# One level of Strassen's scheme for the first expert product, and the experts in 16 units

## The chip, the cores and the metric

The kernel runs on one core of one Trainium2 chip. The metric is the time of one execution on the device in microseconds (us), the median of several runs. Engines are named as in the profile: PE (TensorE, matrix products), PEld (its weight loads), DVE (VectorE), ACT (ScalarE), POOL (GpSimd) and SP (SyncE, which issues most transfers).

## What is computed

Attention of 2 batches and 8 heads of 64 over 1152 positions, with queries averaged in pairs, and behind it four experts whose outputs are weighted and summed:

```python
q_pool = q.reshape(B, H, S // 2, 2, D).mean(axis=3)
attn = softmax(q_pool @ k.T / sqrt(D))          # 2 x 8 heads, 576 x 1152
x = (attn @ v) as 1152 rows of 512              # row = batch and position, column = head and unit
p = domain_probs / domain_probs.sum(-1)
for e in range(4):
    h = np.maximum(x @ w1[e], 0.0)              # 512 -> 1024
    out += p[:, e:e + 1] * (h @ w2[e])          # 1024 -> 512
```

All is float32. A product is made of float32r operands: each factor is split into a high half (a rounded copy) and a low half (what the rounding left), and three products are summed: high by high, high by low, low by high.

## The kernel before

**Heads.** The heads are taken in 8 pairs: n = 0 to 3 are the pairs hp = 0 to 3 of batch 0, n = 4 to 7 those of batch 1. A pair has 9 tiles of 128 query rows (i = 0 to 8; 72 tiles g = 9 n + i in all). The loop over g (L426) gives each engine its instructions in this order: the transposes of tile g (T_chunk, L286) with their copies to aT by ACT (L295) and DVE (L293); the exponentials of tile g+1 on ACT (exps, L272); a part of the product with v (PV_part, L308, into po); the preparation of the next pair's q and k; the scores of tile g+2 (S_chunk, L263) with the scaling on DVE (neg_scores, L266, into sx); then the entries of STAGES. Engines run their instructions strictly in the order in which they are written.

A pair's tiles fall into two groups, grp 0 (256 columns) and grp 1 (320). When the last part of a group's v product is there, finish (L334) multiplies it on DVE by the reciprocal row sums rb into x, copies x to xh on ACT and makes the low half xl on POOL. rb comes from diag_sums (reciprocals on DVE, then dg on POOL, L320 and L324) and spread_sums, a product on PE (pr, L331) that waits for dg. diag_sums of grp 1 stands at i = 8, its spread_sums at i = 1 of the next pair.

**Weights.** w1 and w2 come in 16 half-matrices of 512 x 512. load_weights (L65) issues two transfers on SP for one, split_weights (L103) makes the high half (L98, tensor_scalar) and the low half (L101, tensor_tensor) on POOL.

**Experts.** The rows of x are cut into three chunks of 384. For each expert and chunk, mm1 (L495, matmuls in mm1_ft at L92) goes over 8 slices of 128 FF units with 12 matmuls of 384 columns each (four parts of the inner dimension, three half products), and ACT (L94) and DVE (L95) make the halves of the hidden units. mm2 (L505, matmuls at L515) makes three tiles of 128 rows, each of 24 matmuls of 512 columns over the whole FF dimension, which DVE weights and adds into acc (L518, L520). There are 12 such steps. mm1 of a step is written ahead of mm2 of the step before it. So there are 1152 matmuls of 384 columns and 864 of 512 (the last tile is done in two halves of 256).

**The transition.** mm1 of the first expert and chunk is cut into 32 pieces of three matmuls (fill, L418, tile p1t): four pieces at i = 7 of the last pair, four at i = 8, four behind the loop, and the rest behind the last spread_sums and PV_part. gate_weights (L404) makes the expert weights pw on DVE there.

Of the kernel before, what the change touches and what calls it, by code (L numbers as in the profile page):

```python
# [17 lines left out]
def attention_moe_kernel(ctx, tc, q, k, v, probs, w1, w2, out):  # L18
# [35 lines left out]
    wslot.append(q2all[:, :4096].rearrange("p (z c f) -> p z c f", z=2, c=4))  # L54
    identr = const.tile([P, P], F32R, name="identr")
    nc.vector.tensor_copy(identr, ident)

    stage = [
        kn.rearrange("p h t d -> p (h t d)"), qn.rearrange("p t r d -> p (t r d)"),
        stg, qs.rearrange("p t r d -> p (t r d)"),  # L60
    ]
    stage = [t[:, :1024].rearrange("p (c f) -> p c f", c=2) for t in stage]
    order = [(e, w, hf) for e in range(E) for w in (1, 2) for hf in range(2)]

    def load_weights(j):  # L65
        src = weight_src(*order[j])
        for c in range(2):
            nc.sync.dma_start(stage[2 * (j % 2) + c], src[:, 2 * c:2 * c + 2, :])

    def raw_piece(j, kt):  # L70
        return stage[2 * (j % 2) + kt // 2][:, kt % 2, :]

    ha = [
        k2[0].rearrange("p h s -> p (h s)"), khl.rearrange("p h t z d -> p (h t z d)"),
    ]
    ha = [t[:, j * NC:(j + 1) * NC] for t in ha for j in range(6)]
    ha += [q2all[:, 4096 + j * NC:4096 + (j + 1) * NC] for j in range(4)]
    hbufs = [(ha[0:8], ha[8:16])]
    where = {order[0]: wslot[0], order[1]: wslot[1]}

    seq = [(e, c) for e in range(E) for c in ((0, 1, 2) if e < E - 1 else (0, 2, 1))]

    def mm1_ft(e, c, ft, pt, part=None):
        hh, hl = hbufs[seq.index((e, c)) % 2]
# [482 lines left out]
```

## Time and profile before

| | us |
|---|---|
| median of 3 runs | 682.6 (682.49 to 683.42) |
| profiled execution, span of its instructions | 682.3 |
| PE busy | 663.2 (97%) |
| DVE, ACT, POOL busy | 257.9, 226.1, 201.4 |
| chain that ended last: PE, DVE, ACT | 90%, 4%, 4% |
| share of that chain: w2 products (L515) | 29% |
| x.w1 in the expert stage (L92, tile p) | 27% |

The heads end near 284 us; from there to the end the experts run. PE's busy time is that of a pipelined engine, whose records overlap: the time that a stream of matmuls takes is read from the start of one block to the start of the next, not from the mean duration of one. A wait is read from the idle time ahead of an instruction and the releaser named behind it.

### The profile page before, as it was taken

Reading aid. Unit: us, or ns where it says so; the run is one execution under the profiler, and the core shown is the slowest. Engines: PE = TensorE matmul, PEld = TensorE weight load, DVE = VectorE, ACT = ScalarE, POOL = GpSimd, SP = SyncE. Lnnn points to the kernel's source line nnn. Section 1 sums busy time; section 2 is a strip of 40 time slices with the busy share of each in tenths; the row PEclk is TensorE's granted clock in tenths of the full one; section 3 lists DMA queues with packets and bytes.
Section 4 is the critical chain, followed back from the end, with each engine's and each line's share of the span. In section 5 each row is a group of like instructions: output and inputs, shape, how many; then the busy total and the mean of one; then the engine's idle time right before and its main releaser. Section 6 shows DMA issues by size and latency. Waiting matters only on the chain.

```text
span 682.3 us, 11118 instructions
## 1 busy us (share of the span) xinstructions
PE 663.2 (97%) x4634; PEld 553.6 (81%) x4634; DVE 257.9 (38%) x453; ACT 226.1 (33%) x402; POOL 201.4 (30%) x242
## 2 busy tenths in 40 slices
PE   6899999999999999999999999999999999999998
PEld 5667676767676766798989898989898989898987
DVE  4666666667665765221212121212121212121211
ACT  3666676666666665120101010101020202020200
POOL 3224233332323515391250080440160530310000
PEclk7899999999999999999999999999999999999999
DMA  6715362717172931031030030020030100001011
GB/s 207 197 43 140 96 181 57 202 37 201 39 199 75 239 110 62 1 124 62 2 123 1 0 115 10 31 93 1 0 124 1 42 21 1 0 1 33 14 43 51
DMA packets 26451, 50.84 MB, mean 75 GB/s; under 512 B 2464, under 2 KB 9888, under 8 KB 26400
## 3 DMA queue, kind: packets, MB, share of 16 engines
q1 hardware_dynamic: 26400, 50.12, 26.1%
q8 instruction: 37, 0.61, 0.4%
q14 instruction: 14, 0.11, 0.1%
HBM read 30.97 MB, written 2.36 MB: 49 GB/s over the span
## 4 chain that ended last, share of the span: by engine, by line
PE 90%; DVE 4%; ACT 4%; issue 1%; POOL 0%; ACTq 0%; POOLq 0%
PE p L515 29%; PE p L92 27%; PE spt L263 10%; PE po L308 10%; PE pt L286 6%; ACT sx L272 3%; DVE sx L266 3%; PE pk L236 2%; PE p1t L92 2%; PE pr L331 1%; PE pq L208 1%; PE warm L363 0%; DVE q2all L203 0%; ACT q2all L201 0%; ACT q2all L181 0%
## 5 line engine op out<-in xcount | busy, mean ns | idle before, releaser
L92 PE MATMUL p<-xh,wslot 128*128 128x384 f32 x640 | 166.8, 339 | 1.2 <-DVE q2all L95 1.2
L266 DVE TENSOR_SCALAR_CACHE_REDUCE sx<-spt 128x1152 f32<-128x1152 f32 x72 | 97.7, 1357 | 64.5 <-PE spt L263 64.2
L92 PEld LDWEIGHTS p<-xh,wslot 128*128 128x128 f32 x640 | 116.7, 188 | 1.9 <-DVE q2all L95 1.5
L92 PE MATMUL p<-xl,wslot 128*128 128x384 f32 x320 | 108.3, 338 | 0.0
L272 ACT ACTIVATE sx<-sx,mn 128x1152 f32<-128x1152 f32 x72 | 90.6, 1259 | 25.3 <-DVE sx L266 22.1
L263 PE MATMUL spt<-k,q2all 128*128 128x384 f32 x384 | 86.3, 361 | 1.4 <-DVE sx L266 1.4
L308 PE MATMUL po<-aT,vn 128*64 128x320 f32 (+1 forms) x576 | 85.0, 418 | 0.0
L94 ACT ACTIVATE hb<-p 128x384 fp32r<-128x384 f32 x48 | 23.6, 492 | 161.4 <-PE p L92 158.3
L515 PE MATMUL p<-wslot,hb 128*128 128x512 f32 (+1 forms) x348 | 75.8, 375 | 0.0
L263 PEld LDWEIGHTS spt<-k,q2all 128*128 128x128 f32 x384 | 66.5, 195 | 10.8 <-DVE sx L266 6.1
L515 PEld LDWEIGHTS p<-wslot,hb 128*128 128x128 f32 x348 | 62.2, 188 | 11.7
L295 ACT ACTIVATE aT<-pt 128x640 f32<-128x640 f32 x72 | 50.7, 705 | 55.9 <-PE pt L286 55.8
L286 PEld LDWEIGHTS pt<-ident,sx 64*128 64x128 f32 x1296 | 48.0, 140 | 26.1 <-issue 8.2
L520 DVE SCALAR_TENSOR_TENSOR acc<-p,pw,acc 128x512 f32<-128x512 f32 (+1 forms) x28 | 20.5, 732 | 124.1 <-PE p L515 124.1
L286 PE MATMUL pt<-ident,sx 64*128 64x64 f32 x1296 | 59.2, 231 | 5.8 <-DVE q2all L203 2.4
L92 PEld LDWEIGHTS p<-xl,wslot 128*128 128x128 f32 x320 | 60.0, 188 | 0.4
L94 ACT ACTIVATE k<-p 128x384 fp32r<-128x384 f32 x30 | 14.8, 492 | 130.6 <-PE p L92 130.6
L95 DVE SCALAR_TENSOR_TENSOR hb<-p,hb 128x384 fp32r<-128x384 f32 x48 | 26.8, 558 | 78.1 <-ACT hb L94 78.1
L98 POOL TENSOR_SCALAR wslot<-stg 128x512 fp32r<-128x512 f32 x12 | 7.5, 622 | 161.6 <-PE p L92 84.0
L348 POOL TENSOR_TENSOR xl<-xs,xh 128x256 fp32r<-128x256 f32 (+2 forms) x20 | 13.4, 678 | 133.1 <-ACT xh L347 133.1
L515 PE MATMUL p<-wslot,k 128*128 128x512 f32 x168 | 51.9, 390 | 0.0
L308 PEld LDWEIGHTS po<-aT,vn 128*64 128x64 f32 x576 | 35.3, 136 | 20.3
(107 smaller groups left out, 779.7 us busy)
## 6 DMA issues: line engine op xcount, KB each, us to landing
kab<-k SPq DMA_DIRECT2D x32, 288.0 KB, 4.6
q2all<-q2all SPq DMA_DIRECT2D x28, 256.0 KB, 5.1
vn<-in_v_dram SPq DMA_DIRECT2D x8, 576.0 KB, 7.5
kn<-in_moe_w_dram SPq DMA_DIRECT2D x8, 512.0 KB, 3.7
qn<-in_moe_w_dram SPq DMA_DIRECT2D x8, 512.0 KB, 3.8
stg<-in_moe_w_dram SPq DMA_DIRECT2D x8, 512.0 KB, 3.6
qs<-in_moe_w_dram SPq DMA_DIRECT2D x8, 512.0 KB, 3.9
qn<-in_q_dram SPq DMA_DIRECT2D x7, 576.0 KB, 6.0
```

Of the source, the lines that this page charges most:

```text
L92: nc.tensor.matmul(pt, w[:, a, kt, fs], x[:, kt, cols], start=(j == 0), stop=(j == last))
L94: nc.scalar.activation(hh[ft], pt, AF.Relu)
L95: nc.vector.scalar_tensor_tensor(hl[ft], pt, 0.0, hh[ft].bitcast(F32), ALU.max, ALU.subtract)
L236: nc.tensor.transpose(pt[:, i - f0, :], khl[:, i // KT, i % KT].rearrange("p z d -> p (z d)"), identr)
L263: nc.tensor.matmul(spt[g][:, c, :NC], w, x, start=(j == 0), stop=(j == len(ops) - 1))
L266: nc.vector.tensor_scalar(sx[g % 3].rearrange("p (c x) -> p c x", c=3), spt.pop(g)[:, :, :NC], -INV, None, ALU.mult, ALU.min, accum_out=mn ...
L272: nc.scalar.activation(sx[g % 3], sx[g % 3], AF.Exp, bias=mn[g % 3], scale=-1.0, accum_out=sums[n % 2][:, i:i + 1])
L286: nc.tensor.transpose(pt[:, a, kt - k0, :], sx[g % 3][r, kt * P:(kt + 1) * P], ident[r, r])
L295: nc.scalar.activation(dst, pt, AF.Copy)
L308: nc.tensor.matmul(po[h * HALF:(h + 1) * HALF, :w], vn[n % 2][:, h, kt, :], aT[grp][:, h, kt, :], start=(kt == 0), stop=(kt == KT - 1))
L515: nc.tensor.matmul(pc, h[ft][:, ts_], where[e, 2, ft // 4][:, a, ft % 4, c0:c1], start=(m == 0), stop=(m == len(ops) - 1))
L520: nc.vector.scalar_tensor_tensor(ac, pc, pw[:, tt, e:e + 1], ac, ALU.mult, ALU.add)
```

## The change

**x.w1.** The rows of x are cut into the two batches (576 rows, HT), the inner dimension into heads 0 to 7 by halves (hp 0 and 1, hp 2 and 3), and the FF units of a unit into two slices. That makes x a 2 x 2 matrix of blocks A, w1 of the unit a 2 x 2 matrix B, and seven products of sums of blocks stand for eight (Strassen's scheme in Winograd's form). The sums of x (S1 to S4) are made once, in finish: in pairs 4 to 6 on POOL, in pair 7 on DVE with ACT copies (split_x). The sums of w1 (T1 to T4) are made on POOL for each unit. A product is 12 matmuls of 288 columns: two parts of the inner dimension, three half products, two halves of the 576 rows.

**The chains.** The seven products accumulate in three PSUM tiles of two banks, X, Y and Z. X takes product 0 and, once ACT has copied it (m1), product 2. Y takes product 1 and, once DVE has read it (u1), product 3, then (u2) product 5. Z takes product 4 and, once C22 is read, product 6. C11, C22, C21 and C12 are the four blocks of hidden units, of which ACT, DVE and POOL make the halves.

**Units.** The experts run in 16 units u of two FF slices (j and j+4 of expert e). A unit's mm2 goes over all nine row tiles with six matmuls of 512 columns each and adds each into acc, so acc is added to 144 times. mm1(u+1) is written ahead of mm2(u). Weights come per unit: four transfers for w1, one for w2; ACT makes their high halves, POOL the low ones.

**The transition.** Unit 0 takes the place of fill: product 0 at i = 7, product 2 at i = 8 of the last pair, all others behind the last PV_part. gate_weights moves to pair 1. Tiles of q, k and their preparation are laid into common buffers, which later hold sums of x and the split weights.

```diff
+    HT = NT // 2
+    CW = HT // 2
+    NU = E * 4
...
+    XI = {"S3": 0, "S1": 1, "S2": 2, "S4": 3, "A22": 4}
+
+    def xop(op, z, kt):
+        if op in ("A11", "A12"):
+            return xa[:, int(op == "A12"), z, kt, :]
+        j = XI[op]
+        if kt == 0:
+            return xb[:, j, z, :]
+        if j < 4 or z == 0:
+            return q2all[:, (2 * j + z) * HT:(2 * j + z + 1) * HT]
+        return kk[0][:, 3584:3584 + HT]
...
+    WI = {"B11": 0, "B21": 1, "B22": 2, "T1": 3, "T2": 4, "T3": 5, "T4": 6, "B12": 7}
...
+    def load_w1(u):
+        if u >= NU:
+            return
+        e, j = divmod(u, 4)
+        for a in range(2):
+            src = w1[e, 2 * a * P:2 * (a + 1) * P, :].rearrange("(k p) f -> p k f", p=P)
+            for t in range(2):
+                c = (j + 4 * t) * P
+                nc.sync.dma_start(wf[:, WI[f"B{a + 1}{t + 1}"]], src[:, :, c:c + P])
...
+        g = lambda o: wf[:, WI[o]]
+        for o, a, b in (("T1", "B12", "B11"), ("T2", "B22", "T1"), ("T3", "B22", "B12"), ("T4", "B21", "T2")):
+            nc.gpsimd.tensor_tensor(g(o), g(a), g(b), ALU.subtract)
...
+    WCH = [(0, 2), (2, 4), (4, 6), (6, 7)]
...
+    PRODS = [("X", "A11", "B11"), ("Y", "S2", "T2"), ("X", "A12", "B21"), ("Y", "S3", "T3"),
+             ("Z", "S1", "T1"), ("Y", "A22", "T4"), ("Z", "S4", "B22")]
+
+    def product(u, p, kt, chain, first):
+        _, xo, wo = PRODS[p]
+        for m, (a, z) in enumerate(((0, 0), (0, 1), (1, 0))):
+            for c in range(2):
+                nc.tensor.matmul(
+                    chain[:, c, :CW], w1s[u % 2][:, a, WI[wo], kt, :], xop(xo, z, kt)[:, c * CW:(c + 1) * CW],
+                    start=(first and kt == 0 and m == 0), stop=(kt == 1 and m == 2), skip_group_check=True)
...
+        def split_x(op, kt, c, src, eng):
+            hi, lo = xop(op, 0, kt)[:, c], xop(op, 1, kt)[:, c]
+            if eng is nc.gpsimd:
+                nc.gpsimd.tensor_scalar(hi, src, 1.0, 1.0, ALU.mult, ALU.mult)
+            else:
+                nc.scalar.activation(hi, src, AF.Copy)
+            eng.tensor_tensor(lo, src, hi.bitcast(F32), ALU.subtract)
...
-            x = xs[grp]
+            w, kt = GW[grp], hp % 2
+            c = slice(256 * grp, 256 * grp + w)
+            c1 = slice(HT + 256 * grp, HT + 256 * grp + w)
+            x = xr[:, hp, c1 if b else c]
             nc.vector.tensor_tensor(x, po[:, :w], rb[grp], ALU.mult)
             if b == 0:
-                parts = [(0, 256 * grp, w)]
-            elif grp == 0:
-                parts = [(0, 640, 256)]
+                op = "A12" if hp > 1 else "A11"
+                nc.scalar.activation(xop(op, 0, kt)[:, c], x, AF.Copy)
+                nc.gpsimd.tensor_tensor(xop(op, 1, kt)[:, c], x, xop(op, 0, kt)[:, c].bitcast(F32), ALU.subtract)
+                return
+            a11, a12, a21 = xr[:, kt, c], xr[:, kt + 2, c], xr[:, kt, c1]
+            if hp < 2:
+                nc.gpsimd.tensor_tensor(a11, a11, x, ALU.subtract)
+                if hp == 0:
+                    split_x("S3", 0, c, a11, nc.gpsimd)
+                return
+            eng = nc.vector if hp == 3 else nc.gpsimd
+            eng.tensor_tensor(a11, x, a11, ALU.subtract)
+            split_x("S2", kt, c, a11, eng)
+            eng.tensor_tensor(a21, a21, x, ALU.add)
+            if n == NP - 1 and grp:
+                late.append(lambda: split_x("S1", kt, c, a21, eng))
             else:
-                parts = [(0, 896, 256), (256, 576, 64)]
-            for s0, d0, w in parts:
-                c = slice(d0, d0 + w)
-                nc.scalar.activation(xh[:, hp, c], x[:, s0:s0 + w], AF.Copy)
-                nc.gpsimd.tensor_tensor(xl[:, hp, c], x[:, s0:s0 + w], xh[:, hp, c].bitcast(F32), ALU.subtract)
+                split_x("S1", kt, c, a21, eng)
+            eng.tensor_tensor(a12, a12, a11, ALU.subtract)
+            for op, src in (("A22", x), ("S4", a12)):
+                if n == NP - 1 and grp:
+                    late.append(lambda op=op, src=src: split_x(op, kt, c, src, eng))
+                else:
+                    split_x(op, kt, c, src, eng)
+
+        late = []
...
+            if g == NTL - 1:
+                nc.scalar.activation(UT["m1"], chx[:, :2, :CW], AF.Copy)
...
-            elif i >= 7:
-                fill(4)
+            elif i == 7:
+                chx = ps_s.tile([P, 3, 512], F32, tag="s", name="chx")
+                for kt in range(2):
+                    product(0, 0, kt, chx, True)
+            elif i == 8:
+                for kt in range(2):
+                    product(0, 2, kt, chx, False)
...
+            if (n, i) == (1, 4):
+                gate_weights()
+            if (n, i) == (NP - 2, 2):
+                load_w1(0)
+            if (n, i) == (NP - 2, 4):
+                w1_sums(0)
+            if n == NP - 1:
+                if i == 0:
+                    split_x("S3", 1, slice(0, HT), xr[:, 1, :HT], nc.gpsimd)
+                    load_w2(0)
+                if i < 4:
+                    w1_hi(0, WCH[i:i + 1])
+                    w1_lo(0, WCH[i:i + 1])
+                if i == 3:
+                    load_w1(1)
+                if i == 5:
+                    w1_sums(1)
+        w1_hi(1, eng=nc.gpsimd)
+        w1_lo(1)
+        load_w1(2)
         spread_sums(NP - 1, 1)
         PV_part(NP - 1, 1, 0, KT)
-        gate_weights()
-        fill(32)
-
-    with ExitStack() as mctx:
-        mp = mctx.enter_context(tc.tile_pool(name="mp", bufs=1))
-        ps_m = mctx.enter_context(tc.tile_pool(name="ps_m", bufs=4, space=PSUM))
-        for i in range(3):
-            wslot.append(mp.tile([P, 2, 4, 512], F32R, name=f"wslot{i + 2}"))
-        hb = mp.tile([P, 16, NC], F32R, name="hb")
-        hb = [hb[:, j, :] for j in range(16)]
-        hbufs.append((hb[:8], hb[8:]))
+        chy = ps_t.tile([P, 2, 512], F32, tag="t", name="chy")
+        chz = ps_t.tile([P, 2, 512], F32, tag="t", name="chz")
+        for kt in range(2):
+            product(0, 3, kt, chy, True)
+        nc.scalar.activation(UT["y7"], chy[:, :, :CW], AF.Copy)
+        product(0, 4, 0, chz, True)
+        for fn in late:
+            fn()
+        for kt in range(2):
+            product(0, 1, kt, chy, False)
+        nc.vector.tensor_tensor(UT["u2"], chy[:, :, :CW], UT["m1"], ALU.add)
+        nc.vector.tensor_tensor(UT["u1"], UT["u2"], UT["y7"], ALU.subtract)
+        product(0, 4, 1, chz, True)
+        actx.close()
...
+        def prep_w2(u):
+            if u >= NU:
+                return
+            for sl in range(2):
+                nc.scalar.activation(w2s[u % 2][:, 0, sl], w2f[:, sl], AF.Copy)
+            for sl in range(2):
+                nc.gpsimd.tensor_tensor(
+                    w2s[u % 2][:, 1, sl], w2f[:, sl], w2s[u % 2][:, 0, sl].bitcast(F32), ALU.subtract)
+            load_w2(u + 1)
+
+        def prep_w1(u):
+            w1_hi(u)
+            w1_lo(u)
+            load_w1(u + 1)
...
+        def out_c11(u, chain):
+            hi, lo = hidden(u, "C11")
+            nc.scalar.activation(hi, chain[:, :2, :CW], AF.Relu)
+            nc.vector.scalar_tensor_tensor(lo, chain[:, :2, :CW], 0.0, hi.bitcast(F32), ALU.max, ALU.subtract)
+
+        def out_c(u, name, chain, part):
+            c = UT[name]
+            nc.vector.tensor_tensor(c, chain[:, :, :CW], UT[part], ALU.add)
+            hi, lo = hidden(u, name)
+            nc.scalar.activation(c, c, AF.Relu)
+            nc.scalar.activation(hi, c, AF.Copy)
+            nc.gpsimd.tensor_tensor(lo, c, hi.bitcast(F32), ALU.subtract)
+
+        out_c11(0, chx)
+        out_c(0, "C22", chz, "u2")
+        for kt in range(2):
+            product(0, 5, kt, chy, False)
+        out_c(0, "C21", chy, "m1")
+        for kt in range(2):
+            product(0, 6, kt, chz, False)
+        out_c(0, "C12", chz, "u1")
+        prep_w2(0)
...
+    ps_m = ctx.enter_context(tc.tile_pool(name="ps_m", bufs=1, space=PSUM))
+    ps_2 = ctx.enter_context(tc.tile_pool(name="ps_2", bufs=2, space=PSUM))
...
+    def mm1(u):
+        ch = {n: ps_m.tile([P, 2, 512], F32, tag=n, name="ch" + n.lower()) for n in "XYZ"}
+        done = set()
+
+        def prod(p):
+            n = PRODS[p][0]
+            for kt in range(2):
+                product(u, p, kt, ch[n], n not in done)
+            done.add(n)
+
+        prod(0)
+        nc.scalar.activation(UT["m1"], ch["X"][:, :, :CW], AF.Copy)
+        prep_w2(u)
+        prod(1)
+        nc.vector.tensor_tensor(UT["u1"], ch["Y"][:, :, :CW], UT["m1"], ALU.add)
+        prod(2)
+        out_c11(u, ch["X"])
+        prep_w1(u + 1)
+        prod(3)
+        nc.vector.tensor_tensor(UT["u2"], ch["Y"][:, :, :CW], UT["m1"], ALU.add)
+        prod(4)
+        out_c(u, "C22", ch["Z"], "u2")
+        prod(5)
+        out_c(u, "C21", ch["Y"], "m1")
+        prod(6)
+        out_c(u, "C12", ch["Z"], "u1")
...
+    def mm2(u):
+        e, j = divmod(u, 4)
+        h, w = hb[u % 2], w2s[u % 2]
+        for tt in range(NQT):
+            ts_ = slice(tt * P, (tt + 1) * P)
+            ops = [(sl, a, b) for sl in range(2) for a, b in ((0, 0), (0, 1), (1, 0))]
+            split = u == NU - 1 and tt == NQT - 1
+            for c0, c1 in ((0, 256), (256, 512)) if split else ((0, DM),):
+                pt = ps_2.tile([P, 512], F32, tag="m", name="p2")
+                pc, ac = pt[:, :c1 - c0], acc[:, tt, c0:c1]
+                for m, (sl, a, b) in enumerate(ops):
+                    nc.tensor.matmul(pc, h[:, a, sl, ts_], w[:, b, sl, c0:c1], start=(m == 0), stop=(m == len(ops) - 1))
+                if u == 0:
+                    nc.vector.tensor_scalar(ac, pc, pw[:, tt, e:e + 1], None, ALU.mult)
+                else:
+                    nc.vector.scalar_tensor_tensor(ac, pc, pw[:, tt, e:e + 1], ac, ALU.mult, ALU.add)
...
+    for u in range(NU):
+        if u + 1 < NU:
+            w1_sums(u + 2)
+            mm1(u + 1)
+        mm2(u)
```

## Rows read from the trace of the kernel before

**Rows 1.** The page, parts 1 and 2: PE's busy share and its granted clock.
```profile
PE 663.2 (97%) x4634; PEld 553.6 (81%) x4634; DVE 257.9 (38%) x453; ACT 226.1 (33%) x402; POOL 201.4 (30%) x242
...
PEclk7899999999999999999999999999999999999999
```

**Rows 2.** The chain in order of time: start us, us, engine, tile, line, count.
```profile
278.82 4.84 PE po L308 x36
283.67 10.80 PE p1t L92 x60
295.63 17.22 PE p L92 x96
312.85 16.34 PE p L515 x72
329.18 16.96 PE p L92 x96
...
646.02 33.00 PE p L515 x168
```

**Rows 3.** Timeline 255 to 300 us: start us, us, engine, instruction, [idle before it <-releaser].
```profile
269.80 0.33 PE L92 MATMUL p1t<-xh,wslot 128*128 128x384 f32 x1
...
270.17 0.49 ACT L94 ACTIVATE k<-p1t 128x384 fp32r<-128x384 f32 x1 [1.42 <-PE p1t L92]
...
270.69 0.56 DVE L95 SCALAR_TENSOR_TENSOR khl<-p1t,k 128x384 fp32r<-128x384 f32 x1 [3.00 <-ACT k L94]
...
271.31 0.47 PE L286 MATMUL pt<-ident,sx 64*128 64x64 f32 x8 [0.72 <-DVE khl L95]
...
278.06 0.76 PE L331 MATMUL pr<-dg,ones 128*64 128x320 f32 x4 [1.27 <-POOL dg L324]
```

**Rows 4.** Groups by shape, PE and weight loads: count, busy us, mean ns, idle before.
```profile
L515 PE MATMUL p<-wslot,hb 128*128 128x256 f32 x48 | 5.9, 283 | 0.0
...
L92 PEld LDWEIGHTS p<-xl,wslot 128*128 128x128 f32 x320 | 60.0, 188 | 0.4
```

**Rows 5.** Groups by shape, DVE and ACT.
```profile
L170 DVE TENSOR_TENSOR khl<-kn,khl 128x576 fp32r<-128x576 f32 x1 | 0.8, 759 | 1.3 <-ACT khl L169 1.3
L170 DVE TENSOR_TENSOR khl<-kn,khl 128x256 fp32r<-128x256 f32 x1 | 0.4, 426 | 0.5 <-ACT khl L169 0.5
...
L295 ACT ACTIVATE aT<-pt 128x640 f32<-128x640 f32 x72 | 50.7, 705 | 55.9 <-PE pt L286 55.8
L347 ACT ACTIVATE xh<-xs 128x256 fp32r<-128x256 f32 x12 | 4.8, 403 | 6.6 <-DVE xs L338 6.6
```

**Rows 6.** Windows: length, busy us of PE, PEld, DVE, ACT, POOL, clock, DMA.
```profile
312.60:329.00 16.40, 16.40 (x74) 13.60 (x73) 2.06 (x3) 0.49 (x1) 0.00 (x0) 1.00 0.03 12
346.00:362.50 16.50, 16.50 (x74) 13.65 (x73) 2.06 (x3) 0.49 (x1) 6.11 (x7) 1.00 0.27 85
```

**Rows 7.** Groups by shape, POOL.
```profile
L101 POOL TENSOR_TENSOR wslot<-qn,wslot 128x512 fp32r<-128x512 f32 x14 | 18.0, 1289 | 1.2
...
L348 POOL TENSOR_TENSOR xl<-xs,xh 128x256 fp32r<-128x256 f32 x12 | 8.8, 734 | 104.9 <-ACT xh L347 104.9
L98 POOL TENSOR_SCALAR wslot<-qn 128x512 fp32r<-128x512 f32 x14 | 8.7, 623 | 0.0
```

**Rows 8.** Timeline 238 to 251 us: finish of pair 6, first group, and what follows.
```profile
241.44 0.42 DVE L338 TENSOR_TENSOR xs<-po,rb 128x256 f32<-128x256 f32 x1
...
245.21 0.61 POOL L324 TENSOR_SCALAR dg<-ident,rs 128x128 f32<-128x128 f32 x1
...
247.86 0.71 PE L331 MATMUL pr<-dg,ones 128*64 128x320 f32 x4
```

**Rows 9.** Windows at the start, columns as in rows 6.
```profile
4.00:8.00 4.00, 2.19 (x15) 1.69 (x13) 2.14 (x5) 1.97 (x4) 0.74 (x1) 1.00 0.87 279
8.00:12.00 4.00, 2.89 (x11) 2.45 (x11) 2.28 (x3) 0.85 (x2) 0.80 (x1) 0.56 0.50 152
...
24.00:28.00 4.00, 3.34 (x33) 2.65 (x32) 2.57 (x4) 2.61 (x5) 0.00 (x0) 1.00 0.92 219
```

More of the change, by code (lines that the diff above doesn't have):

```diff
@@ L53, in attention_moe_kernel @@
     q2 = [t[:, :2048].rearrange("p (z s x) -> p z s x", z=2, s=2) for t in q2]
[L54 to L84, printed above, removed]
-        cols = slice(c * NC, (c + 1) * NC)
-        w = where[e, 1, ft // 4]
-        fs = slice((ft % 4) * P, (ft % 4 + 1) * P)
-        ops = [(kt, a, x) for kt in range(NKT) for a, x in ((0, xh), (0, xl), (1, xh))]
-        last = len(ops) - 1
-        for j, (kt, a, x) in enumerate(ops):
-            if part is None or kt == part:
-                nc.tensor.matmul(pt, w[:, a, kt, fs], x[:, kt, cols], start=(j == 0), stop=(j == last))
-        if part is None or part == NKT - 1:
-            nc.scalar.activation(hh[ft], pt, AF.Relu)
-            nc.vector.scalar_tensor_tensor(hl[ft], pt, 0.0, hh[ft].bitcast(F32), ALU.max, ALU.subtract)
@@ new lines, in attention_moe_kernel, with flat, w1_hi, w1_lo @@
+    WCH = [(0, 2), (2, 4), (4, 6), (6, 7)]
+    def flat(t):
+        return t.rearrange("p o k f -> p (o k f)")
+    def w1_hi(u, parts=WCH, eng=None):
+        if u >= NU:
+            return
+        for a, b in parts:
+            dst, src = flat(w1s[u % 2][:, 0, a:b]), flat(wf[:, a:b])
+            if eng is None:
+                nc.scalar.activation(dst, src, AF.Copy)
+            else:
+                eng.tensor_scalar(dst, src, 1.0, 1.0, ALU.mult, ALU.mult)
+    def w1_lo(u, parts=WCH):
+        if u >= NU:
+            return
+        for a, b in parts:
+            nc.gpsimd.tensor_tensor(flat(w1s[u % 2][:, 1, a:b]), flat(wf[:, a:b]),
+                                    flat(w1s[u % 2][:, 0, a:b].bitcast(F32)), ALU.subtract)
@@ new lines, in load_w2 @@
+    def load_w2(u):
+        if u < NU:
+            e, j = divmod(u, 4)
+            nc.sync.dma_start(w2f, w2[e].rearrange("(s j p) d -> j p s d", s=2, p=P)[j])
+    UT = {n: xr[:, (0, 2)[j // 2], (j % 2) * HT:(j % 2 + 1) * HT] for j, n in enumerate(("m1", "u1", "u2", "y7"))}
+    UT |= {n: xr[:, (1, 3, 1)[j], (0, 0, 1)[j] * HT:((0, 0, 1)[j] + 1) * HT] for j, n in enumerate(("C22", "C21", "C12"))}
+    UT = {n: t.rearrange("p (c x) -> p c x", c=2) for n, t in UT.items()}
+    PRODS = [("X", "A11", "B11"), ("Y", "S2", "T2"), ("X", "A12", "B21"), ("Y", "S3", "T3"),
+             ("Z", "S1", "T1"), ("Y", "A22", "T4"), ("Z", "S4", "B22")]
@@ new lines, in attention_moe_kernel @@
+    ov = out.rearrange("(b p t) c -> b t p c", b=B, p=HALF)
+    def mm2(u):
+        e, j = divmod(u, 4)
+        h, w = hb[u % 2], w2s[u % 2]
[10 more added lines that the diff above has]
+                    nc.vector.tensor_scalar(ac, pc, pw[:, tt, e:e + 1], None, ALU.mult)
+                else:
+                    nc.vector.scalar_tensor_tensor(ac, pc, pw[:, tt, e:e + 1], ac, ALU.mult, ALU.add)
+                if u == NU - 1:
+                    for a in range(2):
+                        b, t = divmod(2 * tt + a, NQT)
+                        eng = nc.scalar if split and a else nc.sync
+                        eng.dma_start(ov[b, t][:, c0:c1], acc[a * HALF:(a + 1) * HALF, tt, c0:c1])
```

140 lines of the change are left out of this document (33 added, 107 removed).

## The prediction

> **What bounds the kernel now.** I read the page's busy shares first: PE is busy for 97% of the span and its granted clock is full in every slice but the first two [rows 1]. That can still hide waits, so the chain of waits in order of time comes next. From 295.63 us on it is PE alone, in blocks that follow each other without a gap: 96 matmuls of x.w1 in 16.96 us, 72 of the w2 product in 16.34 us [rows 2]. There are 11 blocks of the first kind after the transition (the first takes 17.22 us) and 12 blocks' worth of the second. So behind 295.63 us only PE instructions count: 176.7 ns for one of 384 columns (16.96/96), 227 ns for one of 512 (16.34/72). Between 265 and 295 us, where the last heads hand over to the experts, the rows show waits: PE stands 1.27 us for POOL's dg and 0.72 us for DVE [rows 3]. This stage has to be walked through by hand. The heads before it (tiles g = 0 to 70) are a loop of PE, DVE and ACT that the change touches only where finish, POOL and the weights go.
>
> **The pace at 288 columns.** The change makes 16 x 84 = 1344 matmuls of 288 columns out of 12 x 96 = 1152 of 384: 387,072 columns for 442,368, seven eighths. The trace has no matmul of 288 columns with 128 x 128 weights. Its nearest rows: 384 columns take 176.7 ns; 256 columns take 120 ns (the last block is 33.00 us for 120 of 512 columns and 48 of 256 [rows 2, 4]: (33.00 - 120 x 0.227)/48 = 0.120). On the line between them 288 columns take 134.2 ns, and that is my value; parallel to the slope between 384 and 512 columns it would be 139 (176.7 - 96 x 0.394), and in proportion to the 227 ns of 512 columns 128. I keep 128 to 139. One x.w1 unit is then 84 x 134.2 = 11.27 us, its w2 product 54 x 227 = 12.26 us, a period of 23.5 us.
>
> Each of these matmuls has its own weight load, and the 48 of 256 columns did too; at 120 ns apiece the load is hidden. The Trainium skill ("TensorE: Matmul & The Clock Gate", Part 3, "The mechanism") says that a weight load overlaps matmuls in flight only where the row groups differ. All loads here take all rows, so by it the 192 additional loads, 188 ns each in the trace [rows 4], would lie bare: +36 us, some 700 us in all. The trace disagrees, since 256 columns and a load fit in 120 ns; I give that a chance under 0.01.
>
> **Units 1 to 15.** They replace 11 blocks: 15 x 11.27 = 169.1 us for 11 x 16.96 = 186.6 us: **-17.5 us**, if PE never waits. The w2 products stay 864 matmuls of 512 columns: 0.
>
> Does PE wait? The chains X, Y, Z are read between products that accumulate into them again. A product is 12 matmuls, 1.61 us. A reader starts some 0.37 us after the last matmul's start (269.80 to 270.17) and PE follows a reader's end by 0.06 us (271.25 to 271.31) [rows 3]. A DVE add of 576 elements takes 0.76 us [rows 5], an ACT copy about 0.65 us (0.70 for 640 [rows 5]). With a unit's start as 0: ACT reads X into m1 from 1.85 to 2.5, product 2 needs it at 3.22; DVE's u1 reads Y from 3.45 to 4.2, product 3 comes at 4.83; u2 reads it from 6.7 to 7.45 (behind the low half of C11), product 5 comes at 8.05; C22 reads Z from 8.3 to 9.05, product 6 comes at 9.66. Every hand-over has about 0.6 us to spare. Behind the unit, the accumulation of the w2 product has 1.36 us a tile (6 x 227 ns) and two banks, against 0.75 us of DVE (three of them, one cut off, are 2.06 us [rows 6]). DVE's 108 more accumulations (144 for 36) lie there too. POOL per unit: four sums of 256, 1792 + 1024 + 1728 columns of low halves at 1.29 us per 512 and 0.73 per 256 [rows 7], about 14.4 us of 23.5. ACT: about 8.6 us. All of it is used one unit later. So I cost these at 0; what is late next, if the cover goes, is the DVE add.
>
> **The heads.** finish of pair 6 (hp = 2, b = 1) puts eleven POOL instructions where there was one (xl, 0.73 us): seven tensor_tensor, four tensor_scalar. At 256 columns that is 7 x 0.70 + 4 x 0.42 = 6.6 us (0.734 a tensor_tensor with its gap hidden; a tensor_scalar between 0.31, half of the 0.62 for 512, and 0.62 [rows 7]). Behind them on POOL stands dg of the second group, and PE's spread (pr) waits for dg with everything behind it. In the trace x is ready at 241.86, dg ends at 245.82, pr starts at 247.86 [rows 8]: 2 us to spare. After: 241.95 + 6.6 + 1.8 (dg) = 250.3: PE stands **+2.4 us** (bounds 0.9, if they run at 0.31 and 0.62, to 3.5). The longer chain of the second group (7.6 us) has 12 us until its dg is needed. gate_weights, moved from the transition to pair 1, is 2 us of DVE in a loop that DVE can hold up: **+0.2** (0 to 1). ACT's four copies for w1_hi in pair 7 fit in its idle time there: 0. The DMAs issued on SP (four of 128 KB per unit, and w2's one) have a period each: 0.
>
> **The transition.** PE in the times of the old trace: product 0 begins where the 12 matmuls of the first filling did (the last of them stands at 269.80 [rows 3], so 269.8 - 11 x 0.177 = 267.8 at the latest) and takes 1.6 us to 269.3; transposes and attention product of the last tile go to some 270.5. Product 2 accumulates into X, which ACT first copies to m1, behind its copy of aT: 271.2. So product 2 is 271.3 to 272.9. Then PE has nothing until pr. In pair 7 finish runs on DVE: x, then seven instructions of 0.43 us with ACT copies of 0.40 between them [rows 5], from 270.95 to 275.7; the sums' reciprocals follow on DVE, dg on POOL, and pr starts at 278.1, as it did (278.06 [rows 3]). But the old kernel had 24 more matmuls to put there: PE now stands for 5.2 us instead of 1.27. pr and the last attention product end at 283.67, as before [rows 2]. Products 3, 4 (first half), 1, 4 (second half) are 36 matmuls, 4.8 us, to 288.5; S2's last low half is ready at 285.9. Product 5 waits until DVE, behind S1, A22 and S4, has read u2: 289.25; product 6 until C22 is read: 291.5 to 293.1. The first unit of the loop starts between 293.1 and 294.2 (a chain's banks may still be read by C12); I take 293.7 for 295.63: **-1.9 us**. The columns saved here (60 matmuls of 8.1 us for 60 of 10.8) mostly turn into waits.
>
> Two costs go on top. First, in both groups of that finish DVE runs seven instructions with both operands in SBUF while POOL works on the sums and halves of w1; the old trace shows no such pair beside each other. Bounds: 0, or one POOL instruction each, 4 x 0.70 in the first group, 4 x 1.29 in the second [rows 7]. Nearest to a row is neither; I take a third, **+2.5 us**. The Trainium skill ("SBUF — State Buffer", on the shared port pair) says that DVE and GpSimd lock one port pair for a whole instruction and that the loser blocks; by it the sum would be nearer the upper end, +6. No row here shows it. Second, the clock. Its mean was 0.56 from 8 to 12 us, after 4 us in which PE was busy for 2.19, and 1.00 again from 24 us [rows 9]; later waits of 0.7 to 1.3 us did not lower it [rows 1, 3]. A stand of 5.2 us is longer than any in the trace. At the half level (1.2 instead of 2.4 GHz) the attention product behind it (4.84 us) would take up to twice as long. **+2.0 us** (0 to 5).
>
> **Sum**, against the profiled span: -17.5 + 2.4 + 0.2 - 1.9 + 2.5 + 2.0 = -12.3 us on 682.3 us: 670.0. The median of the runs is 0.3 us above that span: about **670 us**. The tail (last accumulate, two transfers) keeps its length.
>
> **Rivals.**
> (a) No port conflict and no fall of the clock: 4.5 us less, about 665.5. For it: waits up to 1.3 us left the clock alone. Chance 0.22.
> (b) The hand-overs take part of the slack: 0.3 us a unit, or a pace of 138 ns (1260 x 4 ns = 5 us): 673 to 681. Chance 0.20.
> (c) Slower. PE waits in each unit for the DVE reads of the chains (u1, u2, C22). This decides from 12.3/15 = 0.82 us a unit, that is when each of the three reads ends some 0.9 us later than worked out (0.6 spare and 0.27 more). It would come if such an add, one operand in PSUM and one in SBUF, had to wait for a POOL instruction of 1.29 to 1.42 us: three waits of (1.3 - 0.6) make 2.1 us a unit, 670 + 31 = 701; with half of that, 686. Against it: the accumulations, of the same kind of operands, take 2.06 us for three whether POOL is idle or busy for 6.11 us [rows 6]. Chance 0.12.
> (d) The gain vanishes between these, within 0.2%: 0.03.
> (e) A pace near 128 ns and no wait in the transition: below 662. Chance 0.03.
>
> The forecast itself (667 to 673) has 0.40. **Range**: (a), (b) without its upper end and the forecast lie in 662 to 679, about 0.8. A measurement of this kernel can tell about 0.2%, 1.4 us, from no change. Faster by more than that: 0.40 + 0.22 + 0.20 + 0.03 = 0.85; within it 0.03; slower 0.12.
>
> **What the new profile would show.** The product line with 1344 matmuls, 132 to 136 ns from start to start; blocks of 84 in 11.3 us and 54 in 12.3 us in the chain, with no releaser named between them. If DVE adds or POOL stand between blocks, (b) or (c). pr of pair 6 waiting about 2.4 us for dg. A stand of PE of some 5 us ahead of the last pr, and whether the granted clock of the windows behind it falls below 1.00. The first block of 84 starting 3 to 7 us after 293.7. The prediction is wrong if the pace at 288 columns is not on the line between its neighbours, or if any hand-over waits in each of 15 units: 0.1 us there is 1.5 us in the sum.

## The result, and the profile after

The changed kernel takes 674.28 us (674.15 to 676.63), the kernel before 683.01 us (682.49 to 684.11) in the same runs: a ratio of 0.987, interval 0.9849 to 0.9891. It is faster by about 9 us, 1.3%. The forecast was 670, its range 662 to 679. The profiled executions are not the median ones: 674.8 us of span belong to the slowest of four runs (676.63 us, mean granted clock 0.982), while the three others have spans of 672.4 to 672.5 us and clocks of 0.994 to 0.995, and the span of 682.3 us before fits the slowest of its runs, 684.11 us.

The page of the changed kernel, shares and granted clock (the rows of before are [rows 1]):

```profile
PE 644.4 (95%) x4808; PEld 531.2 (79%) x4808; DVE 363.9 (54%) x571; ACT 310.4 (46%) x523; POOL 323.5 (48%) x346
...
PEclk7899999999999999898999999999999999999999
```

PE lost 19 us of busy time, the span only 7.5 (682.3 to 674.8). The 8s in the middle of the clock's row are new. The chain in order of time answers [rows 2]:

```profile
283.54 5.82 PE po L332 x36
...
302.49 2.54 POOL w2s L546 x2
305.05 4.26 DMA qsf<-in_moe_w_dram
312.52 3.12 PE chy L135 x12
315.64 1.85 PE chz L135 x12
317.50 12.28 PE p L625 x54
329.77 1.58 PE chx L135 x12
...
339.36 1.60 PE chz L135 x12
340.96 12.26 PE p L625 x54
```

Two things are to be seen. From 317.5 us on it is PE alone again: seven products in 11.19 us (329.77 to 340.96), the w2 product in 12.26. That pattern holds for units 2 to 15. But in unit 1 the chain leaves PE: it runs over POOL's w2s and a transfer. That unit, from 299.61 (timeline, next) to 317.50, took 17.9 us.

```profile
299.61 1.57 PE L135 MATMUL chx<-xa,kk 128*128 128x288 f32 x10 [0.94 <-ACT hb L569]
```

The waits of PE name what else is new:

```profile
PE pr L355 <- POOL dg L348: 7.2, 2, 4.4
PE chy L135 <- DVE xr L604: 4.7, 1, 4.7
```

So the 7.5 us between the two profiled spans come about like this. The first unit of the loop starts at 299.61 instead of 295.63: +4.0. x.w1 in the loop takes 17.9 + 14 x 11.19 = 174.6 us for 11 blocks with 186.8 us: -12.2. The w2 products stay at 196.2 us. What is left behind the last accumulation grew by some 0.8 us. Together -7.4. The price of the clock is in these numbers, not beside them.

### The profile page after: what moved, and what is told of

Its sections match the earlier page's. It is cut to its first block, busy times and chain, and to the rows that moved or that the text cites. A ratio compares the mean times of both kernels' runs of the same rounds, so it can differ in the third digit from the quotient of the medians.

```text
span 674.8 us, 11945 instructions
## 1 busy us (share of the span) xinstructions
PE 644.4 (95%) x4808; PEld 531.2 (79%) x4808; DVE 363.9 (54%) x571; ACT 310.4 (46%) x523; POOL 323.5 (48%) x346
## 4 chain that ended last, share of the span: by engine, by line
PE 85%; DVE 6%; ACT 5%; POOL 2%; issue 1%; DMA 1%; ACTq 0%; POOLq 0%; DVEq 0%
PE p L625 29%; PE chy L135 11%; PE spt L287 11%; PE po L332 10%; PE chz L135 7%; PE chx L135 7%; PE pt L310 6%; DVE sx L290 3%; ACT sx L296 3%; PE pk L260 2%; PE pr L355 1%; DMA qsf<-in_moe_w_dram 1%; PE pq L232 1%; PE warm L414 0%; POOL xb L364 0%
## 5 line engine op out<-in xcount | busy, mean ns | idle before, releaser
L625 PE MATMUL p<-w2s,hb 128*128 128x512 f32 (+1 forms) x870 | 198.9, 388 | 0.1
L625 PEld LDWEIGHTS p<-w2s,hb 128*128 128x128 f32 x870 | 161.8, 188 | 33.0 <-DVE acc L629 0.3
L629 DVE SCALAR_TENSOR_TENSOR acc<-p,pw,acc 128x512 f32<-128x512 f32 (+1 forms) x136 | 101.5, 746 | 81.6 <-PE p L625 81.6
L287 PE MATMUL spt<-kk,q2all 128*128 128x384 f32 x456 | 101.5, 360 | 1.3 <-DVE sx L290 1.3
L287 PEld LDWEIGHTS spt<-kk,q2all 128*128 128x128 f32 x456 | 79.2, 195 | 11.5 <-DVE sx L290 6.8
L116 POOL TENSOR_TENSOR kk<-kq,kk 128x512 fp32r<-128x512 f32 x64 | 72.0, 1156 | 10.8 <-ACT kk L108 10.8
L570 POOL TENSOR_TENSOR hb<-xr,hb 128x576 fp32r<-128x576 f32 x48 | 68.7, 1435 | 17.3 <-ACT hb L569 17.1
L135 PE MATMUL chx<-xa,kk 128*128 128x288 f32 x384 | 56.4, 296 | 1.5 <-ACT hb L569 0.9
L135 PEld LDWEIGHTS chx<-xa,kk 128*128 128x128 f32 x384 | 53.5, 188 | 3.6 <-issue 1.5
L317 DVE COPY aT<-pt 128x512 f32<-128x512 f32 x72 | 49.0, 680 | 3.6 <-PE pt L310 3.5
```

The lines of the kernel that those rows point to most:

```text
L116: nc.gpsimd.tensor_tensor(flat(w1s[u % 2][:, 1, a:b]), flat(wf[:, a:b]), flat(w1s[u % 2][:, 0, a:b].bitcast(F32)), ALU.subtract)
L135: nc.tensor.matmul(chain[:, c, :CW], w1s[u % 2][:, a, WI[wo], kt, :], xop(xo, z, kt)[:, c * CW:(c + 1) * CW], start=(first and kt == 0 and ...
L287: nc.tensor.matmul(spt[g][:, c, :NC], w, x, start=(j == 0), stop=(j == len(ops) - 1))
L317: nc.vector.tensor_copy(dst, pt)
L570: nc.gpsimd.tensor_tensor(lo, c, hi.bitcast(F32), ALU.subtract)
L625: nc.tensor.matmul(pc, h[:, a, sl, ts_], w[:, b, sl, c0:c1], start=(m == 0), stop=(m == len(ops) - 1))
```

## The experiments

Three waits of PE stand in the trace: 2.8 us for dg of pair 6, 4.4 us for dg of pair 7, 4.7 us in unit 1. Three runs take away one each, by order alone. All times of a kernel are compared by ratio to the kernel before on the same chip (0.987 for the changed kernel), and the spans of the profiled executions by their own rows. A difference of spans compares two single executions, so the ratios say what a move is worth and the rows say where.

### Unit 1's wait: w2 of unit 0 prepared earlier

```diff
         out_c11(0, chx)
+        prep_w2(0)
         out_c(0, "C22", chz, "u2")
...
         out_c(0, "C12", chz, "u1")
-        prep_w2(0)
```

> Only prep_w2(0) is moved: from behind unit 0's last output to behind C11, so that POOL is through with w2's low halves of unit 0, and SP issues the transfer of unit 1's w2, some 8 us earlier. Theory: the 4.7 us for which PE waits in unit 1 (product 5 for u2) is this transfer seen through ACT (w2's copy stands ahead of C11's relu) and DVE (C11's low half stands ahead of u2). Then the wait goes, and with it the fall of the clock behind it: the first unit of the loop takes 11.3 us instead of 17.9, 668 us in all. Rival: the order on ACT and DVE alone does it in the first unit; then the wait stays above 2 us and the time above 671 us.

Measured: 671.87 us (668.59 to 673.1), ratio 0.9812 (0.9776 to 0.9848); span 669.2, 5.6 less. By the ratio it is 4 us less (0.0058 x 683), and the runs lie 4.5 us apart. The expected 668 us, 6.3 less, are reached by unit 1 itself (6.5, below), not by the span and not by the median. The wait for u2 is no longer in the list, and the chain shows unit 1 as PE alone:

```profile
300.45 1.83 PE chx L135 x12
...
310.28 1.60 PE chz L135 x12
311.88 12.26 PE p L625 x54
```

Unit 1 takes 11.43 us (300.45 to 311.88) instead of 17.9: the wait and the low clock behind it were 6.5 us. The rival falls: the same order on ACT and DVE is harmless once the transfer is early. The first unit starts 0.8 us later, though (300.45 for 299.61). POOL's low halves of w2 now lie beside DVE's u1 of unit 0, an add with both operands in SBUF: it takes 1.51 us for 0.76 in the changed kernel, and product 6 of unit 0 waits 1.02 us for 0.27. Timeline of this run:

```profile
294.38 3.03 POOL L546 TENSOR_TENSOR w2s<-qsf,w2s 128x512 fp32r<-128x512 f32 x2 [5.50 <-ACT w2s L544]
294.76 1.51 DVE L531 TENSOR_TENSOR xr<-xr 128x576 f32<-128x576 f32 x1
...
297.66 1.06 PE L135 MATMUL chz<-xb,kk 128*128 128x288 f32 x6 [1.02 <-DVE xr L566]
```

How the wait of unit 1 was passed on is read from the timeline of the changed kernel:

```profile
302.47 2.54 POOL L546 TENSOR_TENSOR w2s<-qsf,w2s 128x512 fp32r<-128x512 f32 x2
...
305.05 7.89 SPq L122 DMA_DIRECT2D qsf<-in_moe_w_dram  x2
...
309.32 1.15 ACT L544 ACTIVATE w2s<-qsf 128x512 fp32r<-128x512 f32 x2 [6.85 <-DMA qsf<-in_moe_w_dram]
...
310.38 0.63 ACT L561 ACTIVATE hb<-chx 128x576 fp32r<-128x576 f32 x1
...
311.04 0.76 DVE L562 SCALAR_TENSOR_TENSOR hb<-chx,hb 128x576 fp32r<-128x576 f32 x1 [7.16 <-ACT hb L561]
311.72 0.75 DVE L604 TENSOR_TENSOR xr<-chy,xr 128x576 f32<-128x576 f32 x1
...
312.52 1.68 PE L135 MATMUL chy<-xb,kk 128*128 128x288 f32 x6 [4.68 <-DVE xr L604]
```

The one buffer of raw w2 is free only when POOL is through with unit 0's low halves (305.01); SP's transfer then lands at 309.3; ACT's copy of w2 stands ahead of C11's relu, C11's low half ahead of u2 on DVE, and product 5 waits for u2. In unit 2 and later the same transfer has a whole w2 product, 12.26 us, to land.

### Pair 6: dg ahead of the sums of x on POOL

```diff
-            eng.tensor_tensor(a11, x, a11, ALU.subtract)
+            if n == NP - 2 and grp == 0:
+                held.append(lambda: sums_x(n, grp, kt, c, x, a11, a12, a21, nc.gpsimd))
+                return
...
             for fn, dn, *args in STAGES.get(i, []):
                 fn(n + dn, *args)
+            while held:
+                held.pop(0)()
```

(sums_x is the rest of finish, unchanged.)

> In pair 6, first group, the eleven POOL instructions of finish are written behind dg instead of ahead of it. Theory: PE's 2.8 us wait for dg goes, and the lower clock behind it (mean 0.67 from 252 to 256 us): 4 us less, 670.3 us. Rival: the loop of the heads gives the time back, because POOL is then late for the second group's dg or the low halves of w1: 1 us less or nothing.

Measured: 673.26 us, ratio 0.984 (0.9825 to 0.9854); span 671.0. The wait for dg of pair 6 is gone; that of pair 7 is where it was:

```profile
PE pr L355 <- POOL dg L348: 4.4, 1, 4.4
```

The first unit of the loop starts at 296.24 in this run's timeline, 3.4 us earlier. The span shows 3.8 us, the ratio 2 us (0.003 x 683), and the intervals of the two ratios overlap (0.9849 to 0.9891 for the changed kernel). The 3.4 us are made of three parts. pr starts 2.9 us earlier (248.09 for 250.98). From pr to X's first product it is 21.0 us here (to 269.13), 21.4 in the changed kernel (to 272.40), where the clock was low behind the wait, and 19.9 in the run of the next section, in which the same wait stands and the clock stayed at 1.00; both runs with all moves, further down, have 21.0 too. So the loop of the heads does give part of the wait back, some 1.1 us (21.0 - 19.9), and the low clock cost some 1.5 (21.4 - 19.9): the rival was right in part.

### Pair 7: dg ahead of DVE's chain

```diff
-            eng.tensor_tensor(a11, x, a11, ALU.subtract)
+            if n == NP - 1 and grp == 0:
+                held.append(lambda: sums_x(n, grp, kt, c, x, a11, a12, a21, nc.vector))
+                return
...
+            while held:
+                held.pop(0)()
```

> In pair 7, first group, DVE's chain of sums is written behind the reciprocals of diag_sums instead of ahead of them. Theory: dg is ready some 4 us earlier, PE's 4.4 us wait shrinks below 0.5 us and the clock behind it stays at 1.00: 6 us less, 668.3 us. DVE's chain now lies beside POOL's work on unit 1's w1 halves. Rival (port conflict): the seven DVE instructions, 0.42 us each while POOL was idle, take up to 1.3 us each beside POOL, S2 comes late, PE waits ahead of product 1, and half of the gain is lost: 671 us.

Measured: 672.16 us, ratio 0.9814 (0.9795 to 0.9833), 3.8 us less; span 668.1. Of the span's 6.7 us, 2.1 are there ahead of the edit: X's first product starts at 270.26 for 272.40. pr of pair 6 accounts for 0.7 of them (250.32 for 250.98); the other 1.5 come behind it, where the clock stayed at 1.00 in this execution (0.67 in the changed kernel's), though PE had waited the same 2.80 us:

```profile
250.32 0.76 PE L355 MATMUL pr<-dg,ones 128*64 128x320 f32 x4 [2.80 <-POOL dg L348]
252.00:256.00 4.00, 4.00 (x52) 2.69 (x51) 2.34 (x4) 2.69 (x5) 3.09 (x4) 1.00 0.25 72
```

(The second line is a window, columns as in [rows 6]; the clock is the number before the last two.) From X's first product to the first unit of the loop (292.45) it is 22.2 us for 27.2: 5.0 us from the edit, expected 6. pr waits 0.89 us instead of 4.38 (expected: below 0.5), the last v product is back at 4.85 us (5.82), and DVE's chain now lies beside POOL. Timeline of this run:

```profile
274.09 0.39 DVE L390 TENSOR_TENSOR xr<-xr 128x256 f32<-128x256 f32 x1
...
274.96 0.84 DVE L364 TENSOR_TENSOR q2all<-xr,q2all 128x256 fp32r<-128x256 f32 x1 [0.48 <-ACT q2all L363]
275.51 1.01 POOL L348 TENSOR_SCALAR dg<-ident,rs 128x128 f32<-128x128 f32 x1
275.72 0.41 DVE L392 TENSOR_TENSOR xr<-xr 128x256 f32<-128x256 f32 x1
...
276.49 2.65 POOL L110 TENSOR_SCALAR kk<-kq 128x512 fp32r<-128x512 f32 x4
276.58 0.76 PE L355 MATMUL pr<-dg,ones 128*64 128x320 f32 x4 [0.89 <-POOL dg L348]
276.62 0.76 DVE L364 TENSOR_TENSOR q2all<-xr,q2all 128x256 fp32r<-128x256 f32 x1 [0.48 <-ACT q2all L363]
...
277.30 0.82 DVE L397 TENSOR_TENSOR xr<-xr 128x256 f32<-128x256 f32 x1
278.05 0.83 DVE L364 TENSOR_TENSOR kk<-xr,q2all 128x256 fp32r<-128x256 f32 x1
```

In the changed kernel the seven instructions, with both operands in SBUF, took 0.42 to 0.43 us each while POOL was idle. Here four take 0.76 to 0.84 us beside POOL's dg and its split of w1 and the last, at 278.80, 0.61; two keep 0.39 and 0.41, and beside the second of these it is POOL's part of dg that takes 1.01 us for 0.60. So the conflict is real, at some 0.4 us an instruction, on one side or the other. DVE's side of it costs nothing visible, since PE has the last v product to do meanwhile. POOL's side falls on dg itself: some 0.4 of the 0.89 us for which pr still waits. Theory and rival each were right in part: the wait is gone but for 0.89 us, the conflict is there, and half of the gain was not lost.

### PE kept busy in the wait

```diff
+        for j in range(30):
+            nc.tensor.matmul(chx[:, 2, :CW], w1s[0][:, 0, 0, j % 2, :], xa[:, 0, 0, j % 2, :CW], ...)
         spread_sums(NP - 1, 1)
```

> Nothing is moved; 30 matmuls of 288 columns whose results nobody reads (third bank of X's tile) are put where PE stands ahead of the last pr. Theory: the wait for dg itself stays, but PE is busy in it and the granted clock stays at 1.00: the last attention product takes 4.84 us again instead of 5.82, and pr 0.8 instead of 1.3: 1.5 us less, 672.8 us. Rival: the clock falls for another reason than PE's standing, and the time stays at 674.3 us or grows.

Measured: 675.64 us, ratio 0.9865 (0.9841 to 0.9889); span 673.6. The windows show what was expected, and a second fall of the clock behind it. First the changed kernel, then this run (columns as in [rows 6]; the clock is the number before the last two):

```profile
252.00:256.00 4.00, 4.00 (x34) 3.06 (x32) 1.56 (x3) 1.81 (x4) 3.54 (x3) 0.67 0.10 29
276.00:280.00 4.00, 1.83 (x12) 1.59 (x12) 2.78 (x9) 1.55 (x4) 0.00 (x0) 1.00 0.00 0
280.00:284.00 4.00, 1.79 (x8) 0.91 (x10) 0.20 (x2) 0.41 (x1) 3.62 (x7) 0.75 0.02 4
284.00:288.00 4.00, 4.00 (x28) 1.98 (x26) 0.00 (x0) 0.03 (x1) 4.00 (x5) 0.83 0.26 76
...
313.00:317.00 4.00, 4.00 (x22) 4.00 (x21) 1.11 (x2) 1.83 (x3) 4.00 (x5) 0.61 0.67 191
```

```profile
280.00:284.00 4.00, 3.57 (x28) 2.67 (x28) 0.42 (x3) 0.44 (x1) 3.40 (x6) 1.00 0.00 0
284.00:288.00 4.00, 4.00 (x31) 1.91 (x27) 0.00 (x0) 0.00 (x0) 4.00 (x5) 1.00 0.23 66
...
308.00:312.00 4.00, 1.61 (x7) 1.61 (x8) 2.18 (x3) 3.45 (x8) 4.00 (x4) 0.63 0.11 12
312.00:316.00 4.00, 4.00 (x19) 4.00 (x19) 0.76 (x1) 2.03 (x3) 4.00 (x4) 0.52 0.77 250
```

With PE busy the clock stays at 1.00, the last v product takes 4.87 us instead of 5.82 and the first unit starts 25.7 us behind X's first product (272.62 to 298.29) instead of 27.2: the expected 1.5 us. So at this place it was PE's standing that lowered the clock, as far as one execution shows it: in the five other traces that keep the wait of 4.38 us the clock fell behind it each time. But behind unit 1's wait, which this run leaves in place, the clock was low for longer than before: the unit took 17.98 us for 17.89, though its wait was shorter (3.88 us for 4.68). What one fall costs is therefore not a constant. Behind pair 7's wait pr and the last v product together took 1.4 to 2.2 us more than the 5.6 us at the full clock, in five traces; unit 1, less its wait and the 11.43 us that it takes without one, lost 1.8 to 2.7 us in four. The span is 1.2 us shorter than the changed kernel's; the medians can't tell the two apart.

### All three moves, and the output on two queues

The edits above together, the two of finish as one:

```diff
+            if n >= NP - 2 and grp == 0:
+                held.append(lambda: sums_x(n, grp, kt, c, x, a11, a12, a21, nc.vector if hp == 3 else nc.gpsimd))
+                return
```

> The three moves together: w2(0) prepared early, dg ahead of finish's sums in pairs 6 and 7. Theory: the three waits lie behind each other in time and add up: 2.8 + 4.4 - 0.9 (left in pair 7) + 4.7 = 11.0 us, and each lowered clock behind them cost 1 to 1.7 us: 14 to 16 us less than the changed kernel, 659 to 661 us, a ratio to the kernel before of 0.965 to 0.968. Rival: removing one wait lengthens the next (POOL is the engine behind all of them): then less than 10 us, above 664 us.

Measured: 661.82 us, ratio 0.9686 (0.967 to 0.9701); span 659.3. Between the two profiled executions the span is 15.5 us shorter; by the ratios the moves are worth 12.6 us (0.0184 x 683), short of the expected 14 to 16, and the median is 0.8 us above the expected 659 to 661. Of the three waits only 0.9 us of pair 7's is left, as expected; product 6 of unit 0 waits 1.06 us for 0.27, as with the early preparation alone; and the granted clock is full behind the start:

```profile
PEclk7999999999999999999999999999999999999999
```

By the ratios the single moves gave 4.0, 2.0 and 3.8 us, 9.8 in all, and together they gave no less. So the waits simply followed each other, and none hid another.

The second kernel also issues every second output transfer of the last unit from ACT:

```diff
-                        eng = nc.scalar if split and a else nc.sync
+                        eng = nc.scalar if a else nc.sync
```

> As the three moves together, and of the last unit's output transfers every second one is issued by ACT instead of SP. Theory: the tail behind the last accumulation is 3.6 us in the changed kernel for 2.8 us in the kernel before because 22 transfers queue up on SP in 12 us (0.68 us each); with half of them the tail is 2.8 us again: 0.5 to 0.8 us less than without it. Rival: the tail is the transfer itself: no difference.

Measured: 661.59 us, ratio 0.9681 (0.9666 to 0.9695); span 659.9. From the end of the last accumulation to the end of the span it is 3.2 us (656.67 to 659.9) for 3.6 without (655.68 to 659.3): 0.4 us less in the traces, less than expected, and not to be told in the medians. The expectation counted 22 transfers; there are 20. It also took 0.68 us for the price of an issue, but that is the pace of the accumulations, two transfers every 1.36 us; a single issue takes 0.47 to 0.54 us. Only at the end does SP fall behind. The last accumulation and the last issue, first in the changed kernel, then here:

```profile
670.76 0.48 DVE L629 SCALAR_TENSOR_TENSOR acc<-p,pw,acc 128x256 f32<-128x256 f32 x1 [0.62 <-PE p L625]
671.76 0.54 SPq L634 DMA_DIRECT2D out_dram<-acc  x1
```

```profile
656.19 0.48 DVE L637 SCALAR_TENSOR_TENSOR acc<-p,pw,acc 128x256 f32<-128x256 f32 x1 [0.63 <-PE p L633]
656.70 0.47 SPq L642 DMA_DIRECT2D out_dram<-acc  x1
```

The last issue starts 0.52 us behind the end of the last accumulation in the changed kernel and 0.03 us behind it here. What makes up the rest of the longer tail stays open. Both kernels beat the changed one by about 12 us and the kernel before by 21.

### The slack of a hand-over

```diff
+        for _ in range(3):
             nc.vector.tensor_tensor(UT["u2"], ch["Y"][:, :, :CW], UT["m1"], ALU.add)
```

> In units 1 to 15 DVE makes u2 three times instead of once (same result), which delays the release of Y by two adds, 1.35 to 1.5 us. Theory: the hand-over has 0.58 us to spare (u2 ends 454.19, product 5 starts 454.83, less 0.06), so PE waits 0.8 to 0.95 us a unit in 14 units: 11 to 13 us more than the changed kernel, 686 us, slower than the kernel before. Rival (no slack, hidden waits in the pace): the whole 1.4 us shows, 20 us more, 694 us.

Measured: 693.31 us, ratio 1.0139 (1.011 to 1.0167); span 691.9, 17.1 more. A unit of the loop:

```profile
460.73 2.34 DVE L605 TENSOR_TENSOR xr<-chy,xr 128x576 f32<-128x576 f32 x3 [0.16 <-PE chy L135]
...
463.13 1.06 PE L135 MATMUL chy<-xb,kk 128*128 128x288 f32 x6 [0.83 <-DVE xr L605]
```

u2 ends 1.58 us later, PE's idle time is 0.83 us, and the period grows from 23.45 to 24.53 us: 1.08 a unit, or 15 us in 14 units. Unit 1 takes 1.1 us more (18.97 us), and 0.8 us stand ahead of it. By the ratios the loss is 18 us. So there is slack, 0.5 us of the 1.58, as expected; but a unit loses 0.25 us more than the idle time named. The first products behind a wait are slower (1.86 us for the twelve of product 5 in the chain of waits, 1.60 elsewhere). The weight loads, which else run ahead, waited too: that is argued as the cause, not shown by a run of its own. The total came out between theory and rival.

### Eight products instead of seven

```diff
         prod(2)
+        prod(2)
         out_c11(u, ch["X"])
```

> Units 1 to 15 make product 2 twice, so that a unit has the 96 matmuls of the plain scheme, with all else of the change in place; the hidden units are then not those of the reference. Theory: behind the transition PE alone decides, so 15 x 1.60 = 24.0 us more than the changed kernel, 698 us; the matmuls saved by Strassen's scheme are the whole gain, and units of 288 columns without it would lose 15 us. Rival: the additional product fills waits or gives other engines time: less than 20 us more.

Measured: 696.03 us, ratio 1.0199 (1.0167 to 1.023); span 698.4, 23.6 more than the changed kernel's; by the ratios it is 22.5 us more. 15 x 1.60 = 24.0 was expected; unit 1's wait shrank meanwhile from 4.7 to 2.7 us, and the period of the units behind it grew from 23.45 to 25.05 us. So behind unit 1 each product is worth its 1.60 us of PE. With 96 matmuls of 288 columns in a unit the kernel is 2% slower than before: the eighth product, which Strassen's scheme saves, is what pays for matmuls of 288 instead of 384 columns and for the waits.

## Why the prediction was right, and where not

**The pace.** Forecast 134.2 ns at 288 columns, measured 11.19/84 = 133.2. The line between 256 and 384 columns held, weight loads stay hidden. Over 15 units that saves 1.2 us more than forecast.

**The hand-overs** in units 2 to 15 cost nothing, as forecast; and the run with three adds bears the slack out. A unit in the timeline of the changed kernel:

```profile
449.88 2.54 POOL L546 TENSOR_TENSOR w2s<-qsf,w2s 128x512 fp32r<-128x512 f32 x2 [8.42 <-ACT w2s L544]
...
450.28 0.76 DVE L599 TENSOR_TENSOR xr<-chy,xr 128x576 f32<-128x576 f32 x1 [2.49 <-PE chy L135]
...
453.43 0.76 DVE L604 TENSOR_TENSOR xr<-chy,xr 128x576 f32<-128x576 f32 x1 [0.16 <-PE chy L135]
...
454.83 0.97 PE L135 MATMUL chy<-xb,kk 128*128 128x288 f32 x6
```

u2 ends at 454.19 and product 5 starts at 454.83, 0.64 us to spare (the run with three adds found 0.5). Rival (c) fell: u1 took its 0.76 us while POOL was at work on w2s. An add with one operand in PSUM took 0.76 us beside POOL and with POOL idle. The mechanism that was weighed, however, turned up for instructions with both operands in SBUF.

**The step that failed** is "All of it is used one unit later. So I cost these at 0", with "The DMAs issued on SP ... have a period each: 0". It holds from unit 2 on. In unit 1 the preparations of two units fall into a few microseconds, since unit 0 has no w2 product in front of its successor; one buffer of raw w2 made SP wait for POOL, and ACT, DVE and PE wait in their orders. It cost 6.7 us (17.9 - 11.2), by the early preparation 6.5. The prediction walks through the steady state and through the transition up to unit 1's first matmul, but not through unit 1 itself.

**dg of pair 6**: forecast +2.4, measured a wait of 2.8 us and a mean clock of 0.67 from 252 to 256 us behind it. The chain on POOL was sized well (its lower bound of 0.9 was not: with tensor_scalar at 0.31, tensor_tensor at 0.62 and the 1.8 us for dg it is 1.5). The low clock behind the wait was put at nothing; it cost some 1.5 us in this execution, while in another with the same wait the clock did not fall. With the longer wait, X's first product stood at 272.40 for 267.75 before: 4.65 us later, where 2.6 were forecast for the heads.

**The transition.** PE's stand ahead of the last pr was forecast as 5.2 us, and there were 4.4 named as waiting (4.68 from the last matmul's start to pr's). The first unit of the loop was forecast for 293.7 + 2.4 + 0.2 + 2.5 + 2.0 = 300.8; it started at 299.6. So the sum came out within 1.2 us, but by terms that offset each other: the heads were 2.0 us worse than forecast (above), and from X's first product to the loop it was 27.2 us for 30.4. There two terms were off: the port conflict (+2.5) did not happen, because POOL was idle during DVE's first chain (0.00 us busy from 276 to 280) and through with w1 when the second began; the clock cost about 1.5 us there (5.82 for 4.84 us, pr 1.34 for 0.76), forecast 2.0. Without these two costs the walk gave 25.9 us, and the trace gives 25.7. The conflict is real all the same: it appeared as soon as a move laid the two engines beside each other, with 0.8 us for 0.4 in pair 7 and 1.51 for 0.76 in unit 0. The Trainium skill ("SBUF — State Buffer", on the shared port pair) says that the loser of the two engines blocks; these rows agree, DVE being the loser in most of them and POOL in one, with 1.01 us for 0.60.

**The tail** was costed at 0 and grew by 0.8 us: all 20 outputs now fall into the last 12 us.

Sum by steps: forecast -17.5 + 2.4 + 0.2 - 1.9 + 2.5 + 2.0 = -12.3 on the span; measured -18.7 + 6.7 (unit 1) + 4.0 (start) + 0.8 (tail) = -7.2, against -7.5 between the spans. The forecast's direction and range held. Its centre was 4 us low, and unit 1 is more than that: the pace (1.2), the conflict that did not happen (2.5) and the cheaper clock in the transition (0.5) paid for part of unit 1, so that the number is nearer than the mechanism, and that is luck. The time lies outside the forecast's own 667 to 673 us and inside the 673 to 681 of rival (b), but not for (b)'s reason: neither the hand-overs nor the pace lost anything in units 2 to 15. These terms are those of the two profiled executions; between the medians it is 8.7 us. A run's time is also 1.8 us above its own span (676.63 for 674.8), so a span of 670.0 would have meant some 671.8 us, not 670.

## What to carry to other kernels

Where a loop is prepared one round ahead, walk through its first round as well as the steady one: there the preparations of two rounds meet, and a single raw buffer ties the engines' orders together. Where PE waits for a short instruction of another engine, see what was written ahead of it on that engine; moving eleven sums behind three instructions gave back 2 us by the ratio and 3.4 us in the trace without any less work. A wait's length is not its price. Unit 1's wait of 4.7 us cost 6.5, with the low clock behind it; of pair 6's 2.8 us the loop of the heads gave 1.1 back. And a move that ends one wait can lay two engines beside each other that had not met: look for what it newly overlaps.
